# Eight one-bank PSUM tiles and halved transform units in a fused long-convolution and MLP kernel

## The chip, the cores and the metric

The kernel runs on one core of a Trainium2 chip. The core has TensorE (PE in the profile, with PEld for its weight loads), VectorE (DVE), ScalarE (ACT), GpSimd (POOL) and SyncE (SP, which issues most DMAs here). The metric is the device time of one execution in microseconds, the median of the runs. The profile shows one execution, whose span runs from the first to the last instruction.

## The reference

Two blocks follow each other on 2048 positions of 640 channels, in bfloat16. The first is a gated long convolution, the second an MLP; both have a layer norm ahead and a residual around them.

```python
def _A_ref(q, k, v, shift_k, ssm_k, ssm_D):
    ...
    for t in range(ks):                                   # ks = 4
        k_shift = k_shift + k_pad[:, t:t + S, :] * shift_k[:, ks - 1 - t][None, None, :]
    kv = k_shift * v
    ...                                                   # FFT convolution of kv with ssm_k, length 2*S
    y = irfft(rfft(kv_pad) * rfft(kf_pad))[:, 0, :S, :]
    y = y + kv * ssm_D[None, None, :]
    return q * y

def _B_ref(x, w1, b1, w2):                                # w1: 640 x 1728, w2: 1728 x 640
    h = jnp.einsum("bsd,df->bsf", x, w1) + b1
    act = h * jnp.tanh(softplus(h))
    return jnp.einsum("bsf,fd->bsd", act, w2)

h = x + _A_ref(_layernorm(x), A_k, A_v, A_shift_k, A_ssm_k, A_ssm_D)
h2 = h + _B_ref(_layernorm(h), B_w1, B_b1, B_w2)
```

## The kernel before

The convolution is done by a two-stage transform with matmuls against tables. The 2048 positions are split as 128 x 16. Channels are worked on in five blocks of 128 (index b or m), which form three chunks: blocks 0 and 1, blocks 2 and 3, block 4.

The stages, by the names that the order uses:

- `k1pe`, `k1ev`, `dadd`: a block of the filter (`d_n`, 512 KB each) is transposed on PE (16 transposes), evicted from PSUM, and the skip term D is added to its first row.
- `ktpe`, `ktev`, `ktsh`: the same for the keys (`d_k`, four loads).
- `kspe`, `kv`: the 4-tap shift as matmuls with banded weights `wsh`, and on DVE the product with v (`d_v`).
- `s1kpe`/`s1kev` and `s1vpe`/`s1vev`: the first transform stage of filter and kv. A unit is eight pairs of matmuls; the two of a pair write PSUM partitions 0 to 63 and 64 to 127 (cosine and sine). One unit fills 1024 fp32 columns, and one eviction empties it.
- `s2kpe`/`s2kev`, `s2vpe`/`s2vev`: the second stage, one matmul for each of 128 frequencies against the table G (`d_g`, eight loads of 512 KB). For the filter all five blocks go in one matmul of 160 columns; for V each chunk has its own, of 64, 64 and 32 columns.
- `sw`: DMAs that copy the filter's transform with rows swapped in pairs; `p2` and `p1`: the products of transforms on DVE.
- `i1pe`/`i1ev`: the first inverse stage, 320 matmuls of 128 columns. `i2pa`, `i2pb`, `i2pc` and `y`: the second, for each tile of 128 positions (t2 = 0 to 15), one matmul pair for each chunk, evicted together as 640 columns.
- `ln1`, `ln1p`, `lnx` (statistics, scale and application of the first layer norm), `wb`, `h` (gate and residual), `bn`, `pow`, `hc` (the second layer norm), then a transpose: on PE for units 0 and 1 (`trpe`, `trev`), by DMA for the others (`trd`).
- The MLP works in five units of 256, 256, 512, 512 and 512 positions. `m1pe` is the first matmul: 14 blocks of 128 inner rows (1728 padded to 1792 with zeros, `w1z`), five matmuls over the channels each; two blocks share a PSUM tile. `hb` is Mish with bias on ACT. `m2pe` is the second matmul, 2 x 14 matmuls of 320 columns for each tile, `res` the residual add on DVE, `d_out` the store.

PSUM is four tiles of 1024 fp32 columns, two banks each, in one ring (`R_PS`) that all stages share. `ev` is the common eviction helper, so all casts from PSUM stand in the profile at line 367 (ACT) or 369 (DVE).

The order of the work is written out by hand as a list, `ORDER`. A word names an operation and its engine: `t` PE, `a` ACT, `v` DVE, `p` POOL, `d` SP's DMA queue (in the changed kernel also `s`, ACT's DMA queue). `_schedule` walks the list once, gives each operation a planned start from the plan's own durations and its dependencies, picks the PSUM tile that comes free first, and the operations are then emitted by planned start; each engine runs its own in that order.

Buffers are shared over time: G's table makes room for w1 and the transposed layer norm, rn (filter blocks) for the swapped copies and then for w2, uv (V's transform) for the MLP's inner values.

Of the kernel before, what the change touches and what calls it, by code (L numbers as in the profile page):

```python
# [11 lines left out]
ALU = mybir.AluOpType  # L12
# [14 lines left out]
d_id:d d_n1:d cz:v d_n2:d wz:v wm:t cfpe:t coef:v k1pe1:t k1pe2:t k1ev2:v warm:a d_n0:d k1ev1:a k1pe0:t k1ev0:v d_n4:d k1pe4:t k1ev4:v kz:p wsh1:p  # L27
dadd1:p dadd2:p s1kpe2_0:t s1kpe2_1:t s1kpe2_2:t s1kev2_1:v d_a12:d d_k2:d dadd4:p s1kpe2_3:t s1kev2_0:a s1kev2_2:a s1kpe4_2:t d_k0:d s1kpe1_1:t
s1kev2_3:a d_n3:d s1kev4_2:v s1kpe4_0:t s1kpe1_0:t d_k1:d d_x0:d s1kev1_1:a dadd0:p wsh3:p s1kpe4_3:t s1kpe0_3:t s1kev4_0:v s1kev1_0:a d_k3:d
s1kev0_3:a s1kev4_3:v s1kpe4_1:t s1kev4_1:a k1pe3:t k1ev3:v ln1_2:v s1kpe0_1:t s1kpe0_2:t s1kev0_1:a s1kpe1_3:t ktpe1_0:t ktpe0_0:t ln1_1:v s1kev0_2:a  # L30
ktpe1_1:t s1kev1_3:a ktpe0_1:t ktpe1_2:t ktpe0_2:t ktpe2_0:t ktpe1_3:t d_v1:d ktpe0_3:t d_g6:d d_v0:d ktev1:v ktpe2_1:t ktpe3_0:t ktev0:a dadd3:p
ktpe2_2:t ktpe3_1:t ktpe2_3:t ktpe4_0:t ktev2:a ktpe3_2:t ln1_3:v ktsh0:p wsh0:p ktpe4_1:t ktpe3_3:t d_g7:d d_g3:d d_g2:d ktpe4_2:t ktpe4_3:t
s1kpe3_3:t ktev3:v s1kpe1_2:t s1kev3_3:a s1kpe0_0:t s1kpe3_0:t s1kev1_2:a ktev4:v ktsh4:p ktsh1:p s1kev0_0:v ln1_0:v s1kpe3_2:t s1kev3_0:a s1kpe3_1:t
kspe0_1:t s1kev3_1:a ln1p0:p kspe0_0:t s1kev3_2:a kspe4_0:t s2kpe_16:t s2kev_16:a kv0_1:v kv0_0:v kspe4_1:t kv4_0:v s2kpe_9:t s2kev_9:a kv4_1:v
kspe1_0:t s2kpe_6:t s2kev_6:a s2kpe_20:t kspe1_1:t d_g5:d d_g4:d d_g0:d ktsh2:p ln1p3:p wsh2:p kv1_0:v ktsh3:p s2kpe_18:t s2kev_20:a s2kpe_17:t
s2kev_18:a kv1_1:v s2kev_17:a kspe3_1:t s2kpe_8:t s2kev_8:a s2kpe_15:t kv3_1:v s1vpe0_3:t s2kev_15:a s1vpe1_0:t kspe3_0:t s2kpe_21:t s1vev0_3:v
s1vev1_0:a s2kpe_14:t kv3_0:v s2kev_21:a s2kpe_13:t s2kev_14:a s2kpe_19:t s2kpe_0:t s2kpe_11:t s2kev_13:v s2kev_19:a s2kev_0:a s2kpe_10:t s2kev_10:a
d_g1:d s2kpe_4:t s2kpe_12:t s2kev_11:v s2kev_4:v s2kev_12:a s1vpe1_1:t s1vev1_1:v s1vpe0_0:t s1vpe0_2:t s1vev0_2:v s1vpe0_1:t s1vpe1_3:t s1vev0_0:a
s1vev0_1:a s1vev1_3:a s1vpe1_2:t s1vev1_2:v s1vpe3_0:t s2kpe_1:t s1vev3_0:a s2kpe_2:t s2kpe_3:t s2kev_2:a s2kev_1:v kspe2_0:t s2kpe_7:t s2kev_3:v
s2kpe_5:t s2kev_7:a kv2_0:v sw0_1:d kspe2_1:t s2kev_5:a s2vpe0_4:t kv2_1:v s2vpe0_7:t s2vev0_4:a s2vpe0_1:t s2vev0_1:a s2vpe0_2:t s2vev0_2:a  # L40
s2vev0_7:v p2_0_4:v s1vpe4_3:t s2vpe0_3:t s2vev0_3:a s2vpe0_5:t s1vev4_3:v s2vpe0_6:t s2vev0_6:a s1vpe3_2:t s1vev3_2:a s2vev0_5:v p1_0_4:v p2_0_5:v
s1vpe2_1:t p2_0_6:v s1vev2_1:v p2_0_7:v s1vpe2_2:t s1vev2_2:a sw0_0:d s1vpe4_2:t s1vpe3_3:t s1vev4_2:a s1vev3_3:a s1vpe3_1:t s1vpe4_0:t s1vev4_0:v
s1vpe2_3:t p2_0_1:v p2_0_2:v s1vpe2_0:t s1vev3_1:a s1vev2_0:a s1vpe4_1:t s1vev2_3:a s2vpe0_0:t s2vpe1_7:t s2vev0_0:a s2vpe1_5:t s2vev1_7:a s2vev1_5:a
s2vpe1_2:t s2vpe1_0:t s2vev1_0:a s2vpe1_4:t s2vev1_4:a s1vev4_1:a p1_0_5:v p1_0_6:v p1_0_2:v p1_0_1:v sw1_0:d p2_0_0:v s2vev1_2:v p2_1_0:v p2_0_3:v
p1_0_0:v sw1_1:d p1_0_7:v p1_0_3:v p2_1_4:v s2vpe1_3:t s2vpe1_6:t s2vpe1_1:t d_x2:d sw2_1:d s2vev1_6:a s2vpe2_3:t s2vev1_3:a p2_1_3:v s2vev1_1:a
s2vev2_3:a s2vpe2_2:t p2_1_7:v p2_1_6:v p1_1_0:v i1pe0_1:t i1ev0_1:a p2_1_5:v p2_1_1:v s2vpe2_1:t s2vev2_1:a s2vev2_2:a sw2_0:d p2_1_2:v p1_1_4:v
p1_1_2:v p1_1_1:v p1_1_3:v p1_1_6:v p1_1_7:v i1pe0_2:t i1pe0_0:t i1ev0_0:a i1pe0_7:t i1ev0_7:a s2vpe2_0:t i1ev0_2:a i1pe0_4:t i1ev0_4:a s2vev2_0:a
i1pe0_6:t i1ev0_6:a i1pe0_3:t p1_1_5:v i1ev0_3:a i1pe0_5:t i1ev0_5:a i1pe1_2:t i1pe1_0:t i1pe1_6:t i1ev1_0:a i1ev1_6:a i1pe1_1:t i1ev1_1:a i1pe1_7:t
p2_2_2:v p1_2_2:v p2_2_3:v d_w11:d d_w13:d i1ev1_2:a i1ev1_7:a p2_2_1:v p2_2_0:v p1_2_1:v p1_2_0:v i1pe1_4:t i1ev1_4:a p1_2_3:v ln1_15:v ln1_11:v
ln1_12:v i1pe2_2:t i1pe1_3:t i1ev2_2:v i1ev1_3:a i1pe2_0:t i1pe2_1:t i1ev2_1:v i1ev2_0:a i1pe1_5:t ln1_13:v d_w14:d d_t2m:d d_w12:d i1pe2_3:t d_x1:d  # L50
i1ev1_5:a d_w10:d d_w2:d i2pa0:t i2pa1:t i2pb0:t i2pa2:t i2pb1:t i1ev2_3:a i2pc0:t y0:a i2pc1:t d_small:p y1:v b1pe:t i2pb2:t ln1p2:p i2pc2:t w1z:p
ln1p1:p gate:p lnx0:p c_b1:a y2:a lnx1:p i2pa9:t i2pa3:t i2pb9:t i2pc9:t y9:a i2pb3:t i2pa12:t i2pc3:t y3:a i2pb12:t i2pa7:t i2pc12:t y12:a i2pb7:t
i2pa4:t i2pc7:t y7:a lnx3:p ln1p15:p lnx2:p wb1:v wb0:v i2pb4:t i2pa13:t h0:v h1:v bn0:v ln1p13:p pow0:p i2pc4:t y4:a bn1:v i2pb13:t i2pa5:t i2pc13:t
y13:a i2pb5:t i2pa14:t i2pc5:t hc0:v i2pb14:t trpe0:t pow1:p y5:a wb2:v hc1:v i2pc14:t y14:a i2pa10:t trpe1:t i2pb10:t trev0:v i2pa15:t wb3:v i2pa11:t
# [12 lines left out]
res9:v hb4_5:a res8:v m2pe14:t m2pe15:t res14:v m2pe13:t d_out7:d d_out9:d d_out5:d d_out11:d d_out1:d res13:v res15:v d_out13:d d_out14:d m2pe12:t
res12:v d_out15:d d_out10:d d_out8:d d_out12:d
# [15 lines left out]
class _Ring:  # L84
    def __init__(self, bufs):
        self.held = [None] * bufs

    def free(self):
        best = None
        for i, rt in enumerate(self.held):  # L90
            t = 0.0
            for u in rt.users if rt is not None else ():
                if not u.done:
                    break
                t = max(t, u.finish + u.lat + _TAIL[u.eng] + _HOP)
            else:
                if best is None or t < best[0]:
                    best = (t, i)
        return best


class _RT:


    def __init__(self, ring):
        self.ring = ring
        self.users = []
        self.tile = None


class _Op:
    def __init__(self, name, opts, deps, allocs, uses, emit, prio, lat):
        self.name = name
        self.opts = opts
        self.deps = [d for d in deps if d is not None]
        self.allocs = list(allocs)
        for rt in list(allocs) + list(uses):
            rt.users.append(self)
        self.emit = emit
        self.prio = prio  # L120
        self.lat = lat
        self.finish = None
        self.start = None
        self.eng = None
# [732 lines left out]
```

## Time and profile before

| | before |
|---|---|
| median of 3 runs | 230.85 us (230.8 to 232.55) |
| profiled execution | 229.75 us |
| its span | 227.9 us |
| granted TensorE clock | 0.999 |
| PE busy | 217.6 us, 2718 matmuls |
| DVE busy | 143.4 us |
| ACT busy | 132.5 us |
| POOL busy | 51.6 us |
| DMA | 30.60 MB |

Busy time of PE counts a matmul from its start to its modelled end; matmuls overlap in the pipeline, so a busy PE need not be at its peak. How fast an engine really works is read from the spacing of starts in an unbroken series. On ACT and DVE, too, one instruction may start while the one before still drains.

### The profile page before, as it was taken

What the parts mean: (1) busy time and instruction counts of PE and PEld (TensorE: products, weight loads), DVE (VectorE), ACT (ScalarE), POOL (GpSimd) and SP (SyncE); (2) the same over time, 40 slices, a digit from 0 to 9 for tenths busy, and PEclk for the clock granted to TensorE, in tenths of its full rate; (3) what the DMA queues carried; (4) which work ended last, traced back from release to release, by engine and by line L of the source; (5) the groups of instructions that cost most, each with busy time, mean ns of one, the idle gap of its engine ahead of it and who ended that gap; (6) DMA issues with size and microseconds to landing.
All of it is one profiled execution on the core that took longest, in us unless ns stands there. A gap on an engine that the chain in (4) does not pass through costs nothing.

```text
span 227.9 us, 6283 instructions
## 1 busy us (share of the span) xinstructions
PE 217.6 (95%) x2718; PEld 164.6 (72%) x2718; DVE 143.4 (63%) x289; ACT 132.5 (58%) x180; POOL 51.6 (23%) x87
## 2 busy tenths in 40 slices
PE   7989999999879999989999999999999999999993
PEld 2889899999768999878877754445567766447772
DVE  0697998999999999899999998810202120002121
ACT  2388979989999999878966004748240004244000
POOL 0550675000000546149852113210000000000000
PEclk9999999999999999999999999999999999999999
DMA  6999991066898495930001421442200100000304
GB/s 189 417 396 423 415 405 39 4 186 171 250 265 237 109 344 183 384 126 1 3 0 29 83 64 20 69 91 58 58 0 3 58 0 3 0 0 1 117 4 169
DMA packets 27086, 30.60 MB, mean 134 GB/s; under 512 B 9201, under 2 KB 23474, under 8 KB 26674
## 3 DMA queue, kind: packets, MB, share of 16 engines
q1 hardware_dynamic: 26944, 30.19, 40.7%
q8 instruction: 21, 0.34, 0.7%
q14 instruction: 7, 0.06, 0.1%
q10 hardware_dynamic: 50, 0.01, 0.0%
q0 software_dynamic: 64, 0.00, 0.0%
HBM read 20.37 MB, written 2.62 MB: 101 GB/s over the span
## 4 chain that ended last, share of the span: by engine, by line
PE 79%; ACT 9%; DVE 5%; DMA 3%; issue 2%; SPq 1%; POOL 0%; DVEq 0%; ACTq 0%
PE ps L807 27%; PE ps L789 27%; ACT uv L367 7%; PE ps L654 4%; PE ps L653 4%; PE ps L460 4%; DMA rn<-in_A_ssm_k_dram 3%; PE ps L566 2%; PE ps L490 2%; ACT uk L367 2%; PE ps L713 2%; PE ps L513 2%; PE ps L461 2%; DVE uv L369 2%; PE ps L602 2%
## 5 line engine op out<-in xcount | busy, mean ns | idle before, releaser
L797 ACT ACTIVATE uv<-ps,b1s 128x512 bf16<-128x512 f32 (+1 forms) x70 | 36.5, 608 | 59.8 <-PE ps L789 59.8
L789 PE MATMUL ps<-G 128*128 128x512 bf16 (+1 forms) x350 | 62.5, 336 | 0.0
L807 PE MATMUL ps<-rn,uv 128*128 128x320 bf16 x448 | 61.8, 299 | 0.0
L807 PEld LDWEIGHTS <-uv 128*128 128x128 bf16 x448 | 43.8, 98 | 17.5
L789 PEld LDWEIGHTS <-G 128*128 128x128 bf16 x350 | 34.1, 98 | 25.8
L367 ACT CAST uk<-ps 128x1024 bf16<-128x1024 f32 (+2 forms) x50 | 46.6, 1093 | 6.3 <-PE ps L461 3.8
L814 DVE TENSOR_TENSOR xa<-ps,xa 128x640 bf16<-128x640 f32 x6 | 4.9, 823 | 49.0 <-PE ps L807 49.0
L367 ACT CAST uv<-ps 128x1024 bf16<-128x1024 f32 x30 | 28.5, 1095 | 0.0
L653 PE MATMUL ps<-a,uv 128*128 128x128 bf16 x160 | 18.7, 219 | 0.0
L653 PEld LDWEIGHTS <-uv 128*128 128x128 bf16 x160 | 17.8, 113 | 0.1
L738 POOL TENSOR_TENSOR r<-ve,mhalf 128x1 f32<-128x1 f32 x16 | 9.5, 595 | 28.5 <-DVE ve L735 28.4
L814 DVE TENSOR_TENSOR xb<-ps,xb 128x640 bf16<-128x640 f32 x6 | 4.9, 823 | 17.1 <-PE ps L807 14.9
L692 POOL TENSOR_TENSOR r<-ve,mhalf 128x1 f32<-128x1 f32 x16 | 12.7, 797 | 6.9 <-DVE ve L688 6.8
L602 PE MATMUL ps<-uv,G 128*128 128x64 bf16 (+1 forms) x384 | 12.6, 187 | 1.7 <-ACT uv L367 1.7
L369 DVE CAST uk<-ps 128x1024 bf16<-128x1024 f32 (+1 forms) x12 | 13.9, 1191 | 0.4 <-ACT uk L367 0.2
L602 PEld LDWEIGHTS <-G 128*128 128x128 bf16 x384 | 11.7, 96 | 2.4 <-issue 2.2
L617 DVE TENSOR_TENSOR uv<-uv,uk 128x1024 bf16<-128x1024 bf16 x20 | 12.6, 688 | 0.1
L519 DVE TENSOR_TENSOR ra<-ps,rb 128x1024 bf16<-128x1024 f32 x10 | 11.7, 1218 | 1.0 <-PE ps L514 1.0
L369 DVE CAST uv<-ps 128x1024 bf16<-128x1024 f32 x10 | 12.0, 1220 | 0.3 <-PE ps L461 0.2
L460 PE MATMUL ps<-cst,ra 128*64 128x128 bf16 x160 | 10.8, 219 | 1.1 <-ACT uv L367 0.8
L461 PE MATMUL ps<-cst,ra 128*64 128x128 bf16 x160 | 11.0, 221 | 0.0
L713 PE MATMUL ps<-uk,ra 128*128 128x256 bf16 (+1 forms) x96 | 10.7, 255 | 0.2
(103 smaller groups left out, 337.3 us busy)
## 6 DMA issues: line engine op xcount, KB each, us to landing
G<-tab_g SPq DMA_DIRECT2D x8, 512.0 KB, 13.5
rn<-in_A_ssm_k_dram SPq DMA_DIRECT2D x5, 512.0 KB, 5.6
ra<-in_A_k_dram SPq DMA_DIRECT2D x4, 640.0 KB, 7.6
rb<-in_A_v_dram SPq DMA_DIRECT2D x2, 1280.0 KB, 11.0
G<-in_B_w_dram SPq DMA_DIRECT2D x5, 432.0 KB, 6.1
rn<-in_B_w_dram SPq DMA_DIRECT2D x1, 2080.0 KB, 11.5
rn<-uk SPq DMA_DIRECT2D x4, 512.0 KB, 6.5
rb<-uk SPq DMA_DIRECT2D x8, 256.0 KB, 7.7
```

What stands on the lines that cost most here:

```text
L367: nc.scalar.copy(o, i)
L369: nc.vector.tensor_copy(o, i)
L460: nc.tensor.matmul(ps[0:64, dgl, :], lhs, mc, start=True, stop=True)
L461: nc.tensor.matmul(ps[64:128, dgl, :], lhs, ms, start=True, stop=True)
L602: nc.tensor.matmul(ps[:, fl * st:fl * st + n], g_v[:, f0 + fl, :], V[c.i][:, :, f0 + fl, :], start=True, stop=True)
L617: nc.vector.tensor_tensor(v, v, K[c.i][:, :, f0:f1, :], ALU.mult)
L653: nc.tensor.matmul(pz[:, dgl, :], V[c.i][:, dg // 4, :, dg % 4], a12[:, 0, :], start=True, stop=False)
L692: nc.gpsimd.tensor_tensor(r1[:, t2:t2 + 1], ve1[:, t2:t2 + 1], mhalf[:, 0:1], ALU.pow)
L713: nc.tensor.matmul(py[:, o:o + w], t2m[:, t2, ri, :], Z[c.i][:, ri * NT + t2, o - c.c0:o - c.c0 + w], start=(ri == 0), stop=(ri == 1))
L789: nc.tensor.matmul(ph[:, i * 512:i * 512 + w], w1[:, dc, fc * P:fc * P + P], lnhT_of(u)[:, dc, 0:w], start=(dc == 0), stop=(dc == NDC - 1))
L797: nc.scalar.activation(hb_of(u)[:, fc, 0:w], rt.tile[:, i * 512:i * 512 + w], ACT.Mish, bias=b1s[:, fc:fc + 1], scale=1.0)
L807: nc.tensor.matmul(po[:, a * 512:a * 512 + 320], hb_of(u)[:, fc, tl * P:(tl + 1) * P], w2[:, fc, a * 320:a * 320 + 320], start=(fc == 0), ...
```

## The change

- **PSUM.** Eight tiles of 512 fp32 columns (one bank each) instead of four of 1024; the ring `R_PS` has eight places.
- **Halves.** A helper `unit` makes each transform unit as two halves, x and y, each with its own PSUM tile, matmuls and eviction. This holds for filter and key transposes, shift, both forward stages and the first inverse stage. In the second inverse stage the first two chunks (512 columns) and the third (128) have their own evictions, `y..a` and `y..b`. The MLP's first matmul evicts each block of 128 rows by itself; the second is two halves of 320 columns for each tile, with two residual adds (448 and 192 columns for the last tile, each stored by itself).
- **V's second stage joined.** Chunks 1 and 2 share one buffer and one matmul of 96 columns for each frequency.
- **Last 64 inner rows.** The 14th block is no longer padded. Its 64 rows are computed for two groups of positions at once, in the two column halves of PE: units 0 and 1 together, the halves of unit 2, units 3 and 4 together (`m1pex`, `hbx`). Its rows of w2 are held twice, for either half (`w2h`), with zeros in the other rows, so the second matmul keeps 14 steps.
- **First filter block in halves.** Block 1 is loaded as two DMAs of 64 partitions and transposed and evicted as two halves (`k1pe1a`, `k1pe1b`).
- **Also in the diff:** the constants `cst` are loaded from ACT's queue instead of SP's; the warm-up has 7 matmuls instead of 10; the products `p1` and `p2` may run on POOL, and six of them (chunk 0) do, each behind a small copy (`turn`) that orders it after DVE's last product; the list is written anew.

Core of the diff:

```diff
-    banks = [psum.tile([P, 1024], F32, name=f"ps{i}") for i in range(4)]
+    banks = [psum.tile([P, 512], F32, name=f"ps{i}") for i in range(8)]
...
-    uv = [big.tile([P, P * c.ng], BF16, name=f"uv{c.i}") for c in CHUNKS]
+    uv = [big.tile([P, P * n], BF16, name=f"uv{i}") for i, n in enumerate((64, 96))]
...
+    def unit(pe_name, ev_name, dur, evs, cols, deps, pe, evf, ns=2):
+        pes, outs = [], []
+        for h in range(ns):
+            rt = _RT(R_PS)
+            x = "xy"[h] if ns == 2 else ""
+            pes.append(OP(pe_name + x, ("pe", dur / ns), ..., allocs=[rt], emit=lambda e, rt=rt, h=h: pe(ps_f32(rt), h)))
+            outs.append(OP(ev_name + x, evs(cols // ns), pes[-1:] + [o_warm], uses=[rt], emit=lambda e, rt=rt, h=h: evf(e, rt.tile, h)))
+        return pes, outs
...
-        for _ in range(10):
+        for _ in range(7):
             nc.tensor.matmul(ps[:, 0:512], wz[:, 0:P], wz[:, P:D], start=True, stop=True)
...
+    def emit_act_dmas(e):
+        nc.scalar.dma_start(cst[:], dram["cst"])
...
+    def emit_kn1(h):
+        return lambda: nc.sync.dma_start(raw_n[1][64 * h:64 * h + 64], A_ssm_k.rearrange("(d m l) s -> m d l s", m=NDC, l=4)[1, 16 * h:16 * h + 16])
...
+            def pe(ps, h, gi=gi):
+                ps = ps.rearrange("p (g f) -> p g f", g=4)
+                for k in range(4):
+                    q = gi * 8 + h * 4 + k
                     lhs = kk_s[dc][:, q * 64:q * 64 + 64] if which else kv_all[:, dc * S + q * 64:dc * S + q * 64 + 64]
+                    nc.tensor.matmul(ps[0:64, k, :], lhs, mc, start=True, stop=True)
+                    nc.tensor.matmul(ps[64:128, k, :], lhs, ms, start=True, stop=True)
...
+    for x, (nf, n) in enumerate(((16, 64), (10, 96))):
+        for f0 in range(0, P, nf):
+            ...
+                    nc.tensor.matmul(ps[:, fl * n:fl * n + n], g_v[:, f0 + h * kf + fl, :], VX[x][:, :, f0 + h * kf + fl, :], start=True, stop=True)
...
+    for x, us in enumerate(((0, 1), (2,), (3, 4))):
+        w = UNITS[us[0]] // (3 - len(us))
+        ...
+                for h in range(2):
+                    rhs = lnhT_of(us[h])[:, dc, 0:w] if len(us) == 2 else lnhT_of(us[0])[:, dc, h * w:h * w + w]
+                    nc.tensor.matmul(ph[64 * h:64 * h + 64, 0:w], w1[:, dc, 13 * P:FF], rhs, start=(dc == 0), stop=(dc == NDC - 1))
...
-            for a in range(2):
-                for fc in range(NFC): ... w2[:, fc, a * 320:a * 320 + 320]
+            for a, (d0, d1) in enumerate(((0, 448), (448, D)) if t2 == NT - 1 else ((0, 320), (320, D))):
+                    for fc in range(NFC - 1):
+                        nc.tensor.matmul(po[:, 0:d1 - d0], hb_of(u)[:, fc, tl * P:(tl + 1) * P], w2[:, fc, d0:d1], start=(fc == 0), stop=False)
+                    nc.tensor.matmul(po[:, 0:d1 - d0], lhs, w2h[:, d0:d1] if h else w2[:, 13, d0:d1], start=False, stop=True)
...
         for o in order:
+            if o.behind is not None and o.behind.probe is not None:
+                nc.gpsimd.tensor_copy(turn[:], o.behind.probe)
```

Parts of the new list that the prediction speaks of:

```diff
+p2_0_2:p p1_0_2:p p2_0_1:p s1vpe4_0y:t ... s2vev0_6x:v p1_0_0:v p1_0_1:v sw0_1:d ...
+... i2pa0:t i2pa1:t i2pb0:t i2pb1:t i2pa4:t i1ev2_2y:v i2pc0:t y0a:a ...
+hc7:v res0a:v trd6:d ln1_13:v lnx10:a m2pe0b:t m2pe3a:t ... m2pe2a:t trd7:d m1pe2_12:t hb2_12:a ...
+m1pe3_11:t m1pex2:t hb3_5:a m1pe4_2:t ... d_out15a:d d_out8:d d_out14:d d_out15b:d
```

More of the change, by code (lines that the diff above doesn't have):

```diff
@@ L43 @@
[L43 to L54, printed above, removed]
@@ L86, in __init__, with when, take @@
         self.held = [None] * bufs
-    def free(self):
[L89 to L99, printed above, removed]
+    def when(self, i):
+        t = 0.0
+        for u in self.held[i].users if self.held[i] is not None else ():
+            if not u.done:
+                return 1e9
+            t = max(t, u.finish + u.lat + _TAIL[u.eng] + _HOP)
+        return t
+    def free(self):
+        t = [self.when(i) for i in range(len(self.held))]
+        i = min(range(len(t)), key=lambda i: t[i])
+        assert t[i] < 1e9
+        return t[i], i
+    def take(self, i, rt):
+        rt.slot = i
+        self.held[i] = rt
 class _RT:
@@ L145, in _schedule @@
     port = fetched = 0.0
+    last = None
     count, mark = 0, _MARK
@@ L171, in _schedule @@
             port = o.finish
+            if eng == "dve":
+                last = o
+            elif o.probe is not None:
+                o.behind = last
         for rt in o.allocs:
-            rt.slot = rt.ring.free()[1]
-            rt.ring.held[rt.slot] = rt
+            rt.ring.take(rt.slot, rt)
         order.append(o)
@@ L293 @@
     b1s = cpool.tile([P, NFC], F32, name="b1s")
+    hbx = cpool.tile([P, 256 + 256 + 512], BF16, name="hbx")
+    w2h = cpool.tile([P, D], BF16, name="w2h")
     gt = big.tile([P, P * P], BF16, name="G")
@@ L474 @@
     p_ops = [[] for _ in CHUNKS]
-    ks_pe_all, kv_ops, s1_k = [], [], {}
+    ks_pe_all, kv_ops, s1_k = [], [[] for _ in range(NDC)], {}
     def chunk_of(b):
```

467 lines of the change are left out of this document (265 added, 202 removed).

## The prediction

> **What bounds the kernel now.** I read the page, then the stretches by stage, the chain that ended last, and single engines' timelines. The page:
>
> ```profile
> PE 217.6 (95%) x2718; PEld 164.6 (72%) x2718; DVE 143.4 (63%) x289; ACT 132.5 (58%) x180; POOL 51.6 (23%) x87
> DVE  0697998999999999899999998810202120002121
> ACT  2388979989999999878966004748240004244000
> ```
>
> The shares mislead: PE's 95% counts the depth of its pipeline, and DVE and ACT are full for the first half and nearly empty in the second. The stretches (length, then busy time of PE, PEld, DVE, ACT, POOL) show two limits:
>
> ```profile
> 9.80:16.00 6.20, 5.93 (x164) 5.49 (x165) 5.92 (x6) 4.35 (x5) 3.21 (x4) 1.00 1.02 403
> 25.00:38.00 13.00, 12.40 (x260) 11.81 (x258) 12.06 (x14) 11.22 (x13) 10.12 (x15) 1.00 0.77 303
> 52.00:69.00 17.00, 14.34 (x426) 13.05 (x423) 17.00 (x24) 17.00 (x20) 0.00 (x0) 1.00 0.88 241
> 134.00:224.30 90.30, 90.25 (x543) 52.95 (x541) 22.41 (x53) 26.27 (x43) 4.99 (x9) 1.00 0.17 41
> ```
>
> Up to 69 us the two engines that empty PSUM (ACT and DVE) set the pace: both are busy 17.00 of 17.00 from 52 to 69, with gaps only before about 45. From 69 on it is PE: first the inverse transform (i1), then, without a gap, the MLP. The chain of waits says the same:
>
> ```profile
> 91.14 1.09 PE ps L713 x10
> ...
> 133.28 23.74 PE ps L789 x110
> ...
> 224.28 0.82 DVE xb L814
> ```
>
> So the span is the time until the second inverse stage (i2) starts, 91.1 us, plus PE's work behind it (131.6 us by my count, 133.1 with its small gaps), plus 3.6 us of tail. I price the change in these three pieces.
>
> **First piece: until i2.** Halves add instructions, not columns. Ahead of i2pa0 the order lists of the diff have 82 evictions on ACT and 39 on DVE before, 159 and 85 after. What one more eviction costs is the part of it that doesn't grow with columns, read from the spacing of starts in full series on ACT:
>
> ```profile
> 39.54 1.08 ACT L367 CAST uv<-ps 128x1024 bf16<-128x1024 f32 x1
> 40.44 1.38 ACT L367 CAST uk<-ps 128x320 bf16<-128x320 f32 x2
> 40.77 1.90 ACT L367 CAST uk<-ps 128x960 bf16<-128x960 f32 x2
> 42.56 2.71 ACT L367 CAST uk<-ps 128x960 bf16<-128x960 f32 x3
> 43.41 1.86 ACT L367 CAST uk<-ps 128x960 bf16<-128x960 f32 x2
> ```
>
> 1024 columns hold ACT 0.90 us (39.54 to 40.44), 320 hold it 0.33 (to 40.77), 960 hold it 0.85 (42.56 to 43.41), though each shows a longer duration: one starts while the last drains. The line through them is 0.07 us plus 0.81 ns a column, so 512 columns should cost 0.485 us and a split 0.07. No cast of 512 columns is in the trace; below, the split can't cost less than nothing, and the far end is the nearest row of that shape, the Mish of 512 columns (L797): eight in 4.73 us with 0.69 for the last, 0.577 each. I take the line, since it is the same operation. DVE by the same reading: six L519 in 6.88 us with 1.22 for the last, 1.13 each for 1024 columns; a 640-column cast 0.74 (119.32 to 120.06); so 0.09 fixed. Added: 77 x 0.07 = 5.4 us on ACT and 46 x 0.09 = 4.1 on DVE.
>
> Taken off DVE in this piece: six products of chunk 0 go to POOL, 6 x 0.60 = 3.6 us (L617 and L621 in series), and three statistics (ln1_12, ln1_13, ln1_15) go behind i2, 3 x 1.23 = 3.7. Sum over both engines 9.5 - 7.3 = +2.2, or **+1.1 us** on each.
>
> The start: cst leaves SP's queue for ACT's, so the first filter block is issued at 0.73 instead of 1.15, **-0.4 us**. Its halves make the first transposes earlier too, but the new order does the transposes of all four first blocks ahead of the first transform unit, as before, and those blocks arrive at the pace of the DMA engines, busy 0.98 of 3 to 9.8 us. So the halves themselves I price at nothing; the cover is that load stream. The second set of 16 weight loads (1.08 us more on PE) is hidden there too. The shorter warm-up (7 for 10 matmuls, 1.3 us) goes with the block's earlier arrival.
>
> What finer units should buy is idle time. Between 9.8 and 91 us (81.2 us) the stretches add up to 75.3 us busy on ACT and 77.1 on DVE, so 10 us of idle, 5.0 on each, nearly all before 52. The waits name it: ACT for PE at L461, at L566 and at the change from one transform to the next, DVE for L514 and for the last filter block. With eight tiles an eviction can begin after four column pairs, not eight, and PE may run seven units ahead instead of three; the order fills the change of transforms with key transposes. Bounds: nothing gained (the gaps are late loads and dependencies) and all 5.0. I take half, **-2.5 us**.
>
> V's joined second stage saves 128 of 384 matmuls: 64 of the 32-column ones take 1.88 us, so 128 cost 3.8, while widening the 64-column ones to 96 adds about 2. The 1.8 us are worth nothing while ACT and DVE are full (52 to 69); if that cover went, they would be a gain. The i1 stage stays as long as it was: 320 matmuls at 0.0556 us (two rows of L653 start 0.11 apart with one of L654 between) are 17.8 us, plus 1.3 us of V's remainder instead of two groups of 0.80. So i2 is earlier only if i1 starts earlier. Sum of this piece: 1.1 - 0.4 - 2.5 = **-1.8 us**, bounds +0.7 and -4.3.
>
> The queues that move: the weight loads d_w1 still wait for the last second-stage matmul; d_x1 now stands behind d_w2 on SP, which has one more transfer of 80 KB. It then lands some 5 us after i1 ends; its first user, ln1_4, has 10.9 us of DVE work ahead of it from i2's start. Hidden, with about 6 us to spare. On POOL, d_small and the w2h memset come ahead of the six products; POOL sat idle from 37 to 76 us.
>
> **Second piece: PE behind i2.** The 14th block of 64 rows now costs 5 matmuls in each of five units: 2 x 5 x 0.109 + 3 x 5 x 0.216 = 4.33 us (ten L789 of 256 columns take 1.09, twenty of 512 take 4.32). As column pairs it costs half, if a pair runs at once. The first transform shows that such pairs do:
>
> ```profile
> 11.05 0.22 PE L460 MATMUL ps<-cst,x 128*64 128x128 bf16 x1
> 11.05 0.22 PE L461 MATMUL ps<-cst,x 128*64 128x128 bf16 x1
> 11.10 0.22 PE L460 MATMUL ps<-cst,x 128*64 128x128 bf16 x1
> ```
>
> Both halves start together and the next pair 0.055 us later, the pace of one matmul of 128 columns. That saves 2.16 us. Going in and out of the halves costs about 0.09 each time (last transpose at 10.81, first pair at 10.97, where 0.067 was its pace), six times, 0.5. Net **-1.6 us**, bounds 0 and -2.2. [...]
>
> The second MLP matmul stays 448 long; its halves are the same two runs of 14. The residual adds double to 32 at 320 columns: 16 x 0.09 = 1.4 us more on DVE, which is under 2 tenths busy there. What could be late is the layer norm of tiles 4 to 7 that m1pe2 waits for: before, its last DMA transpose is issued by 130.5 us and lands about 2.6 later, m1pe2 starts at 133.28, so it is just in time. In the new order DVE has 30.8 us of work from i2 to hc7 instead of 33.9, PE 38.4 instead of 40.7: the margin grows by about 1 us. I price it at nothing; late DVE would show as a PE gap there, microsecond for microsecond. m1pex2 waits for tiles 12 to 15; m1pe4 and all that PE has left queue behind it, but other m1pe4 blocks stand ahead of it and wait for the same tiles.
>
> **Third piece: the tail.** PE ends at 224.28 and the span at 227.9: 0.82 us of residual add over 640 columns, 0.33 of issue, the rest landing. The last piece is 192 columns now: 0.09 + 0.195 plus the drain, about 0.4 us. With the smaller transfer **-0.6 us**, bounds -0.4 and -0.9.
>
> **Sum:** -1.8 - 1.6 - 0.6 = -4.0 us on a span of 227.9, so 223.9, and 225.75 for the profiled execution (229.75; 1.85 lie around its span). The runs have a median of 230.85, 1.1 above the profiled one; I carry that over: **226.85 us**, 1.7% less. A measurement here tells about 1% from no change.
>
> **Rivals.**
>
> (1) All idle goes: the engines run full from about 11 us on, as they do from 52 to 69. Another -2.5: 224.3 us. For it: no wait over 0.7 us after 45 us even with four tiles. Against: filter blocks and G still come by a full DMA stream until 34 us.
>
> (2) The halves buy no idle time, because the gaps are late loads and the drain between stages. Then the first piece is +0.7 and the sum -1.5: 229.35 us, no change that can be told.
>
> (3) POOL is late. Six products there cost about 1.9 us each (2.07 for 1120 columns, L417), 11.4 in a row, and DVE, in order, stops at p1_0_1, which needs the last of them; behind it queue the products of chunk 0 that i1 waits for and evictions of V. The list leaves DVE 7.1 us of work from the first to there. If POOL starts no earlier than the list has it, DVE loses 11.4 - 7.1 = 4.3 us: 231.15. Against: the swapped copy of K that POOL needs is issued some 11 us of work before, so POOL can start 3 us sooner. POOL's own exposure is real in the trace:
>
> ```profile
> 76.79 4.00 POOL L692 TENSOR_TENSOR r<-ve,mhalf 128x1 f32<-128x1 f32 x1
> ```
>
> This takes 0.55 us elsewhere and stood still while DVE multiplied. But the order keeps DVE on PSUM casts meanwhile, and those kept their 1.13 us beside POOL's L417 at 13.2.
>
> (4) **Slower:** a half doesn't follow the line. If a cast of 512 columns holds ACT 0.577 us, as the Mish does, ACT pays 159 x 0.092 = 14.6 us more ahead of i2, of which 2.5 fit into its remaining idle time: +12.1, 239 us. The forecast's gain is used up from 0.041 us a half, (4.0 + 2.5)/159. Against: four widths lie on one line, and Mish carries a bias operand. [...]
>
> (5) The pairs don't overlap at 256 and 512 columns: 2.2 us lost, 229 us.
>
> **Chances.** Forecast 0.5, (1) 0.25, both faster by over 1%. (2) 0.11, (3) 0.05, (5) 0.02 within 1%. (4) 0.07. That gives faster 0.75, same 0.18, slower 0.07. The range runs from all bounds met at once (-4.3 - 2.2 - 0.9 = -7.4: 223.4), a little under it for a first half that packs tighter than counted, to rival (3): 222.5 to 231.2.
>
> **What would show it.** Right: i2 (the first matmul on t2m) starts near 89.3; series of 512-column casts on ACT 0.49 apart; ACT and DVE together idle some 5 us between 10 and 89; the 64-column pairs of the MLP starting together; from the first MLP matmul to the last no gap on PE over 1 us; 3 us from PE's end to the span's. Wrong: casts over 0.53 apart (rival 4), DVE waiting for POOL before i1 (3), a PE gap ahead of unit 2's first MLP matmul, or i2 at 91 or later with the casts as priced (2).

## The result, and the profile after

The changed kernel takes 228.87 us (median of 20 runs, 227.55 to 230.67) against 230.53 for the kernel before on the same chip: a ratio of 0.9925, 95% interval 0.9902 to 0.9948. That is 0.75% less, where 1.7% less was forecast. The interval leaves out no change at all, but the difference is under the 1% that the prediction named as what a measurement can tell. Its profiled execution has a span of 226.4 us (before: 227.9).

The page of the changed kernel, the totals and the slices of DVE and ACT:

```profile
PE 216.7 (96%) x2608; PEld 164.9 (73%) x2608; DVE 149.0 (66%) x351; ACT 133.8 (59%) x266; POOL 63.3 (28%) x94
DVE  0489799999999999888999898675820000002422
ACT  2188699999999999899786025730206357400000
```

ACT has 266 instructions where it had 180, and DVE 351 where it had 289: the halves. From 28 us to about 85 both digits stand at 9; before, a few 7s and 8s stood among them up to 51 us. The first six slices together are no fuller than before. The stretches shown in the prediction, now:

```profile
9.80:16.00 6.20, 6.20 (x130) 6.04 (x130) 4.55 (x11) 4.64 (x7) 3.27 (x5) 1.00 1.02 408
25.00:38.00 13.00, 12.73 (x255) 12.45 (x254) 12.43 (x23) 12.05 (x25) 2.33 (x4) 1.00 0.82 316
52.00:69.00 17.00, 15.91 (x389) 14.34 (x386) 16.93 (x31) 17.00 (x37) 15.84 (x10) 1.00 0.71 193
134.00:223.30 89.30, 89.28 (x554) 52.67 (x552) 30.48 (x82) 26.03 (x42) 8.25 (x15) 1.00 0.18 43
```

After the stretch come PE, PEld, DVE, ACT and POOL busy with their counts, the granted clock, the DMA share and GB/s. Between 25 and 38 us ACT is 0.8 us fuller, but between 9.8 and 16 us DVE has 4.55 busy us where it had 5.92. A window that overlaps the second stretch lost more; before first, then after:

```profile
20.00:30.00 10.00, 9.40 (x197) 8.97 (x198) 9.20 (x21) 9.28 (x10) 4.29 (x6) 1.00 1.01 413
```

```profile
20.00:30.00 10.00, 7.97 (x216) 7.57 (x211) 8.52 (x15) 8.07 (x18) 7.33 (x14) 1.00 0.88 330
```

PE, DVE and ACT are all less busy there. The chain of waits of the changed kernel has the three marks of the prediction: the first matmul on t2m (L788), the first MLP matmul (L883), and the last work on PE (L900).

```profile
93.12 3.08 PE ps L788 x30
...
101.68 3.87 PE ps L883 x35
...
220.22 1.77 PE ps L900 x13
```

i2 starts 2.0 us later than before (93.12, was 91.14). PE's last matmul ends at 223.28 (before: 224.25), so its stretch behind i2 is 130.16 us, 2.95 less. The tail is 3.11, 0.58 less. Sum: +1.98 - 2.95 - 0.58 = -1.55, the whole difference of the spans. **So the pieces behind i2 brought what was forecast and more; the piece ahead of it, forecast at -1.8, went the other way.**

### The profile page after: what moved, and what is told of

It reads as the page before. It is cut to its first block, busy times and chain, and to the rows that moved or that the text cites. A ratio compares the mean times of both kernels' runs of the same rounds, so it can differ in the third digit from the quotient of the medians.

```text
span 226.4 us, 6281 instructions
## 1 busy us (share of the span) xinstructions
PE 216.7 (96%) x2608; PEld 164.9 (73%) x2608; DVE 149.0 (66%) x351; ACT 133.8 (59%) x266; POOL 63.3 (28%) x94
## 4 chain that ended last, share of the span: by engine, by line
PE 81%; ACT 8%; DVE 4%; DMA 2%; issue 2%; SPq 1%; ACTq 0%; DVEq 0%
PE ps L883 25%; PE ps L900 25%; ACT uv L415 6%; PE ps L788 4%; PE ps L523 4%; PE ps L728 3%; PE ps L645 3%; PE ps L729 3%; DVE uv L417 3%; PE ps L619 3%; PE ps L550 2%; DMA rn<-in_A_ssm_k_dram 2%; ACT uk L415 2%; PE ps L901 2%; PE ps L569 2%
## 5 line engine op out<-in xcount | busy, mean ns | idle before, releaser
L900 PE MATMUL ps<-rn,uv 128*128 128x320 bf16 (+2 forms) x416 | 61.0, 299 | 0.0
L883 PE MATMUL ps<-G 128*128 128x512 bf16 (+1 forms) x325 | 58.9, 337 | 0.0
L900 PEld LDWEIGHTS <-uv 128*128 128x128 bf16 x416 | 40.5, 98 | 16.8
L415 ACT CAST uk<-ps 128x512 bf16<-128x512 f32 (+1 forms) x91 | 47.5, 706 | 3.1 <-PE ps L524 2.6
L883 PEld LDWEIGHTS <-G 128*128 128x128 bf16 x325 | 31.2, 98 | 23.6 <-issue 0.6
L415 ACT CAST uv<-ps 128x512 bf16<-128x512 f32 (+2 forms) x63 | 33.2, 859 | 0.0
L906 DVE TENSOR_TENSOR xa<-ps,xa 128x320 bf16<-128x320 f32 x12 | 5.5, 484 | 40.4 <-PE ps L901 40.4
L417 DVE CAST uk<-ps 128x512 bf16<-128x512 f32 (+1 forms) x32 | 20.1, 678 | 1.3 <-ACT uk L415 0.4
L574 DVE TENSOR_TENSOR ra<-ps,rb 128x512 bf16<-128x512 f32 x20 | 12.5, 684 | 0.2
L417 DVE CAST uv<-ps 128x512 bf16<-128x512 f32 (+1 forms) x19 | 11.8, 681 | 0.0
L645 PE MATMUL ps<-uk,G 128*128 128x160 bf16 x128 | 11.5, 230 | 0.0
L415 ACT CAST rb<-ps 128x512 bf16<-128x512 f32 (+1 forms) x26 | 11.0, 475 | 0.9 <-PE ps L788 0.7
L523 PE MATMUL ps<-cst,ra 128*64 128x128 bf16 x160 | 11.1, 219 | 0.3
```

The lines of the kernel that those rows point to most:

```text
L415: nc.scalar.copy(o, i)
L417: nc.vector.tensor_copy(o, i)
L523: nc.tensor.matmul(ps[0:64, k, :], lhs, mc, start=True, stop=True)
L574: nc.vector.tensor_tensor(kv_w[:, m, :, 8 * h:8 * h + 8, l0:l0 + n], ps.rearrange("p (l t d) -> p d t l", l=n, t=8), raw_v[:, 8 * h:8 * h ...
L645: nc.tensor.matmul(ps[:, o:o + 160], g_v[:, f, :], KA[:, :, f, :], start=True, stop=True)
L883: nc.tensor.matmul(ph[:, 0:w], w1[:, dc, fc * P:fc * P + P], lnhT_of(u)[:, dc, 0:w], start=(dc == 0), stop=(dc == NDC - 1))
```

## The experiments

The question was what made the start 3.8 us worse than forecast. All ratios are to the kernel before. For each profiled execution the table splits the time until i2 in two: the work is half of what ACT and DVE are busy until then, the idle time is the rest. "First pair" is the start of the first pair of the first transform.

| kernel | ratio (95%) | first pair | i2 starts | work | idle |
|---|---|---|---|---|---|
| before | 1 | 10.97 | 90.98 | 79.23 | 11.75 |
| changed | 0.9925 (0.9902 to 0.9948) | 13.13 | 92.96 | 80.22 | 12.73 |
| changed, ten warm-ups | 0.9909 (0.9885 to 0.9933) | 10.97 | 92.71 | 80.16 | 12.55 |
| changed, whole first block | 0.9817 (0.9795 to 0.984) | 10.84 | 91.40 | 79.98 | 11.42 |
| whole, ten warm-ups | 0.9818 (0.9796 to 0.9841) | 10.75 | 91.16 | 80.04 | 11.12 |
| the same, 32 more instructions | 0.985 (0.983 to 0.9871) | 10.70 | 91.61 | 80.02 | 11.59 |
| the same, transfer in halves | 0.9878 (0.9857 to 0.99) | 11.34 | 92.28 | 80.06 | 12.22 |
| the same, V's load late | 0.9769 (0.9749 to 0.9789) | 11.09 | 90.41 | 79.95 | 10.46 |
| before, with halves alone | 1.0082 (1.0059 to 1.0104) | 11.38 | 93.88 | 82.90 | 10.98 |

(Here i2 is the first matmul of its line, 0.16 us ahead of the chain's entry.)

**Ten warm-up matmuls.** The transposes of the changed kernel run slowly at the start:

```profile
1.26 3.17 PE L443 MATMUL ps<-hc 128*128 128x512 bf16 x7 [1.26 <-DVE warm L433]
4.56 2.22 PE L604 MATMUL ps<-cst,rn 64*128 64x64 bf16 x32
7.73 1.94 PE L619 MATMUL ps<-cst,rn 128*128 128x128 bf16 x16 [0.95 <-DMA rn<-in_A_ssm_k_dram]
```

Sixteen whole transposes take 1.94 us, 0.107 apart, and the first pair of the first transform comes 2.2 us later than before. The first suspect was the warm-up:

```diff
-        for _ in range(7):
+        for _ in range(10):
             nc.tensor.matmul(ps[:, 0:512], wz[:, 0:P], wz[:, P:D], start=True, stop=True)
```

> The changed kernel with ten warm-up matmuls in place of seven; nothing else differs. Theory (clock): seven matmuls, 32 quarter-array transposes and a wait of 1 us leave TensorE at half rate, so the whole-block transposes run 0.105 us apart and the first pair of the first transform starts at 13.1 us. With ten they should run about 0.067 apart, the first pair should start near 11.2, the first matmul on t2m near 91.5 in place of 93.1, and the time should fall by 1 to 2 us below the changed kernel (ratio to the kernel before about 0.985). Rival (front off the path): filter blocks and G come by a full DMA stream to 34 us, so the earlier start is lost in later waits: the first matmul on t2m moves by under 0.4 us, ratio 0.9925 as without it. Rival (halving): the split of the first block costs by itself; the transposes stay at 0.105.

```profile
5.64 1.98 PE L604 MATMUL ps<-cst,rn 64*128 64x64 bf16 x32
7.55 1.21 PE L619 MATMUL ps<-cst,rn 128*128 128x128 bf16 x16
8.70 0.20 PE L463 MATMUL ps<-sk_r,cst 32*128 32x80 bf16 x1
```

The same sixteen take 1.21 us, and the first pair starts at 10.97 as before. But i2 moves by 0.25 us and the ratio by 0.0016, inside both intervals. The theory was right on the transposes and wrong on the time: of 2.2 us gained at 11 us, 0.4 are left at 30. What takes them is a wait of PE on nothing that the profile shows. The two stops of this kernel:

```profile
22.75 0.96 PE L550 MATMUL ps<-cst,ra 128*128 128x128 bf16 x13 [1.50 <-issue]
...
29.22 0.98 PE L550 MATMUL ps<-cst,ra 128*128 128x128 bf16 x13 [1.66 <-issue]
```

The changed kernel's own stops are 1.76 us (to 24.54) and 0.27 (to 29.64), so 1.1 of the 2.2 us go into longer stops.

**Seven warm-up matmuls in the kernel before.** The edit is the reverse, in the old kernel.

> The kernel before with seven warm-up matmuls in place of ten; nothing else differs. Theory (clock): the transposes of the filter blocks (0.067 us apart) slow to about 0.1, the first pair moves from 10.97 to 12.5 or later, and the time rises by 1 to 2 us (ratio 1.004 to 1.009). Rival (front off the path): ratio 1.000 +- 0.002, though the transposes may be slower. Rival (halving): the transposes stay at 0.067, ratio 1.000.

Ratio 1.0044 (1.0016 to 1.0071), 1.0 us; by the medians 0.4 (231.2 against 230.81). Its 64 filter transposes, in one row, start at 5.48 and take 5.80 us. They are 0.107 apart until 8.8 us and 0.062 from there on, yet the first pair comes only 0.24 later. By the ratio the loss lies at the foot of the clock theory's range, by the medians below it; a slow start of the transposes is not free there, but its price stays uncertain.

**The first filter block whole again,** with seven and with ten warm-up matmuls:

```diff
-d_go:d d_n1a:d wz:v wm:t d_n1b:d d_n0:d ... k1pe1a:t k1pe1b:t ... k1ev1a:v k1ev1b:v dadd1b:v ... dadd1a:p
+d_go:d d_n1:d wz:v wm:t d_n0:d ... k1pe1x:t k1pe1y:t ... k1ev1x:v k1ev1y:v ... dadd1:p
```

> The changed kernel with the first filter block whole again (one transfer, two units of eight 128x128 transposes, one addition of the D row), still with seven warm-up matmuls. Theory (clock, too few warm-up matmuls): still about 0.1 us a transpose, first pair near 13, ratio near 0.9925. Rival (halving: 64x64 transposes keep TensorE cold): transposes at 0.067, first pair near 11.3, ratio about 0.985.

> The changed kernel with ten warm-up matmuls and the first filter block whole: the start as it was before, everything else changed. Theory (clock): transposes at 0.067, first pair near 11, the first matmul on t2m near 91 to 91.5, ratio about 0.985; if the halves of the first block were worth anything, it is slower than ten warm-ups with the halved block by up to 1 us. Rival (front off the path): 0.9925.

0.9817 and 0.9818: the halved block costs about 1% (2.3 to 2.5 us by the medians, 226.35 and 226.6 against 228.87), and with the block whole the number of warm-up matmuls makes no difference. With seven of them the first pair starts at 10.84, not near 13: the transposes are 0.107 apart only until 6.0 us, where in the changed kernel it is until 12.8. So seven warm-up matmuls by themselves don't explain the late start; each of these is one execution, and what sets the moment stays open.

The place of the stops explains part of the 1%. With the whole block and ten warm-ups:

```profile
22.54 0.24 PE L523 MATMUL ps<-cst,xa 128*64 128x128 bf16 x1 [1.30 <-issue]
...
27.06 0.30 PE L644 MATMUL ps<-uk,G 128*128 128x160 bf16 x2
28.67 2.53 PE L644 MATMUL ps<-uk,G 128*128 128x160 bf16 x34 [1.30 <-issue]
```

Count PE's instructions in the order up to each stop, a matmul and its weight load as one each. With the halved block the first stop comes with 13 of the 16 transposes of ktpe2y and ktpe0y left: after 700 instructions. With the whole block it comes three matmuls into s1kpe0_3x: 700 as well. The second comes after 956 (13 of 24 transposes of ktpe left) and 954 (two matmuls into the second stage). So PE stops at the same instruction, 256 apart (within the two of the count), whatever it executes; the 32 instructions that the halves add (16 transposes and 16 weight loads) push work from ahead of the stop to behind it. The second stage of the filter starts at 27.06 with the whole block and at 30.04 with the halved one. The page of the changed kernel lists a queue for instructions:

```profile
q8 instruction: 20, 0.33, 0.6%
```

Twenty packets of 16 KB; the kernel before, with 220 more instructions on PE, has 21. From 99.20 us on, where PE has no wait in the changed kernel, the packets start 242 to 258 of PE's instructions apart, so one goes with each such step. A stop lasts 1.3 to 1.7 us in the versions of the changed kernel with ten warm-ups and a DMA share of 1.0 from 20 to 30 us.

**32 more instructions and nothing else,** and **the transfer in halves and nothing else,** both on the kernel with ten warm-ups and the whole block:

```diff
-        for _ in range(10):
+        for _ in range(7):
             nc.tensor.matmul(ps[:, 0:512], wz[:, 0:P], wz[:, P:D], start=True, stop=True)
+        for _ in range(19):
+            nc.tensor.matmul(ps[:, 0:80], wz[:, 0:P], wz[:, P:P + 80], start=True, stop=True)
```

> The changed kernel with the first filter block whole and ten warm-up matmuls, of which the last three (1536 columns) are cut into 19 of 80 columns (1520 columns): 32 more instructions on TensorE (16 matmuls and their weight loads, as many as the halved block adds) in about the same time. Theory (code delivery: while the DMA stream is full, TensorE gets its instructions in blocks of some 250, one in about 6.3 us, and stops at the same instruction numbers, near 700 and 945, whatever it executes): the two stops come 32 instructions earlier in the program, the first second-stage matmul of K starts near 30.0 us in place of 27.1 with a stop at 28.7, the first matmul on t2m about 1.3 us later (92.4), ratio to the kernel before 0.988 against 0.982. Rivals (the transfer in halves, or the half transposes themselves, cost the time): the same as without, 0.982.

```diff
-d_go:d d_n1:d wz:v wm:t d_n0:d
+d_go:d d_n1a:d wz:v wm:t d_n1b:d d_n0:d
```

> The changed kernel with ten warm-up matmuls, the first filter block transferred in two halves of 64 rows but transposed whole. Theory (code delivery): as with the whole transfer, ratio 0.982, the first matmul on t2m near 91.2. Rival (the halved transfer costs: by 25 us the changed kernel had moved 0.3 MB less than the one with the whole block): the later blocks land about 0.7 us later, the first matmul on t2m near 92.5, ratio 0.988 to 0.991.

```profile
21.87 1.02 PE L551 MATMUL ps<-cst,ra 128*128 128x128 bf16 x13 [1.69 <-issue]
...
28.07 1.01 PE L551 MATMUL ps<-cst,ra 128*128 128x128 bf16 x13 [1.31 <-issue]
```

With 32 cheap instructions added, the stops fall into the same transposes with the same number left as in the halved kernel: again after 700 and 956. That settles what the stops count. The price of 32 instructions was over-guessed: 0.985, 0.7 us by the ratio (0.0032; the intervals overlap) and 0.45 us at i2, not 1.3; the second stage starts at 28.92, not 30.0. The stops ended 0.6 to 0.7 us earlier than without (21.87 for 22.54, 28.07 for 28.67), which gave part of it back.

The halved transfer alone gives 0.9878, 1.4 us more than whole, with i2 1.1 later; the code theory had expected nothing. The two kernels' first 9 us, halves first:

```profile
0.00:9.00 9.00, 6.38 (x44) 3.59 (x45) 2.20 (x5) 1.56 (x3) 0.20 (x4) 1.00 0.80 247
```

```profile
0.00:9.00 9.00, 7.13 (x53) 4.23 (x54) 2.31 (x5) 2.17 (x3) 0.61 (x5) 1.00 0.79 270
```

At the same busy share the engines moved 247 GB/s instead of 270, that is 0.2 MB less in 9 us, or half a microsecond at the 408 of the full stream (changed kernel, 9.8 to 16 us); the first pair starts 0.6 later. One pair of traces would be little, but the other versions of the changed kernel agree: in the same window the two others with halves have 256 and 258 GB/s, the seven others with the transfer whole 263 to 284. Why transfers of 64 rows are slower there was not tried.

**Halved transposes alone,** the transfer whole, on the changed kernel with ten warm-ups (its `k1pe1a` and `k1pe1b` wait for one `d_n1`):

```diff
-d_go:d d_n1a:d wz:v wm:t d_n1b:d d_n0:d
+d_go:d d_n1:d wz:v wm:t d_n0:d
```

> The changed kernel with ten warm-up matmuls and the first filter block transferred whole, but transposed in two halves of 16 transposes of 64x64 each, as the change has it. With the transfer also whole in its transposes the ratio was 0.982, with both halved 0.991. Theory (three costs add: the halved transfer 0.9 us, 32 more instructions 0.4 us, the rest the 16 more transposes' own time): 2.3 - 0.9 = 1.4 us over the whole block, ratio 0.988. Rival (the halves cost only together, by the wait between them): ratio 0.984 or less.

0.9864 (0.9832 to 0.9895), 1.1 us over the whole block. The intervals overlap, but on the same chip all six runs (227.23 to 228.51 us) lie above all four of the whole block (226.09 to 226.64). With the transfer's 1.4 this makes 2.5, against 2.1 for both by the ratios (0.9909 - 0.9818): they add, within the intervals. So each half of the edit costs something by itself. How much of the transposes' part is the 32 instructions (0.7 above) and how much their own time is not separated. In its profiled execution the granted clock is 0.50 from 22.8 to 26.1 us, behind a stop of 1.96, so its i2 start is not in the table.

**V's load behind x's.** On the kernel with the whole block and ten warm-ups:

```diff
-... d_g6:d s1kev2_3x:a s1kev3_2y:a d_v1:d s1kpe0_2y:t ... d_x0:d s2kpe_12x:t
+... d_g6:d s1kev2_3x:a s1kev3_2y:a s1kpe0_2y:t ... d_x0:d d_v1:d s2kpe_12x:t
```

> The changed kernel with the first filter block whole and ten warm-up matmuls, and the load of the first half of V (1.28 MB, some 3.2 us of the DMA stream) moved on SP's queue from 17 us to behind the load of x at 27 us. Theory (code delivery slowed by the full DMA stream): the stream ends some 3 us earlier, near 23.7, so the stop of 1.3 us at 28.7 goes and the first one at 22.5 may shorten; the first matmul on t2m 0.8 to 1.3 us earlier (near 90.1), ratio about 0.977. Rival (the stops have another cause, or V is then late): no gain, or a wait of kspe for V after 31 us; ratio 0.982 or above.

The same window before and after this edit:

```profile
23.00:30.00 7.00, 5.70 (x139) 5.47 (x134) 5.17 (x9) 5.86 (x11) 1.90 (x4) 1.00 1.02 396
```

```profile
23.00:30.00 7.00, 7.00 (x164) 6.91 (x159) 6.20 (x11) 6.84 (x14) 2.23 (x4) 1.00 0.67 235
```

With the DMA share down to 0.67 PE has no idle time there; the second stop is gone and the first is 1.13. The ratio is 0.9769 as expected, the i2 start 90.41 (expected 90.1). With a median of 225.34 us this is the fastest version, ahead of both kernels.

The traces also hold every DMA packet with its queue and its start, which ties the stops to the code directly. Start and end of the second and the third packet of q8, and the moment at which PE goes on behind instruction 700 and behind about 956:

| kernel | second packet | PE goes on | third packet | PE goes on |
|---|---|---|---|---|
| changed | 22.01 to 23.09 | 24.54 | 27.32 to 28.38 | 29.64 |
| changed, ten warm-ups | 20.20 to 21.28 | 22.75 | 26.69 to 27.75 | 29.22 |
| whole, ten warm-ups | 20.00 to 21.09 | 22.54 | 26.17 to 27.18 | 28.67 |
| the same, 32 more instructions | 19.49 to 20.52 | 21.87 | 25.55 to 26.62 | 28.07 |
| the same, V's load late | 20.44 to 21.53 | 22.76 | 24.84 to 25.94 | no stop |

Every stop ends 1.2 to 1.5 us after a code packet has landed. In the three middle rows, under the full stream (a DMA share of 1.0), the third packet starts 3.6 to 3.9 us after PE goes on behind 700; with V's load late (0.67 from 23 to 30 us) it is 2.1, and the packet has landed 1.5 us before PE comes to that place, at 27.43. So it is the code that PE waits for, and at the second stop the full stream that makes it late. What a packet waits for before it starts is not shown.

With seven warm-up matmuls instead:

> The changed kernel with the first filter block whole and V's load behind x's (ratio 0.977 with ten warm-up matmuls), with seven. Theory (the start is paced by code blocks, so a cold TensorE at 5 us is hidden): the same, 0.977 +- 0.002. Rival (clock: with the stops shortened the cold start shows): slower by 0.5 to 1 us, ratio 0.980.

0.9801 (0.9771 to 0.983); the intervals overlap, so whether the shorter warm-up costs time again once the stops are shorter stays open. In its profiled execution the transposes of the filter are 0.062 apart from their first on, so it had no slow start, and still i2 starts 1.3 us later, at 91.73.

**The halves alone in the kernel before:** its list with each unit as two neighbours, V's later stage not joined, no pairs, the whole block.

```diff
-s1kpe1_3:t ... s1kev1_3:v
+s1kpe1_3x:t s1kpe1_3y:t ... s1kev1_3x:v s1kev1_3y:v
```

> The kernel before with the eight one-bank tiles and every transform unit in halves, and nothing else of the change: its order with each unit as two adjacent halves, V's later stage not joined, the 64 rows padded, the first block whole, ten warm-up matmuls. Theory (a half costs what the line through the widths says, and the idle time of ACT and DVE is late loads and code, not the size of a unit): 123 added evictions at 0.07 and 0.09 us are 9.5 us of two engines, 4.8 each, of which some is taken from idle time: the first matmul on t2m 2 to 4 us later, ratio 1.010 to 1.018. Rival (finer units let the two engines run full): the idle time pays it, the first matmul on t2m within 1 us of before, ratio under 1.005.

1.0082, 1.9 us slower, i2 2.9 later: between the two expectations. The work per engine grows by 3.67 us, 7.3 engine-us for 123 added evictions, 0.06 each, where the prediction had 0.07 and 0.09. The idle time falls by 0.77 us.

**The column pairs taken back,** on the fastest version:

```diff
-        for fc in range(NFC - 1):
+        for fc in range(NFC):
...
-m1pex0:t hbx0:a
+m1pe0_13:t m1pe1_13:t hb0_13:a hb1_13:a
```

> The changed kernel with the first filter block whole, ten warm-up matmuls and V's load behind x's (ratio 0.977), with the last 64 inner rows padded to a 14th block again as before: 25 matmuls in five units in place of 30 that run as column pairs. Theory (a pair runs in the time of one): 4.33 us in place of 2.54, so TensorE's stretch from the first matmul on t2m to its last grows by 1.8 us, from 130.3 to 132.1, the start stays as it is, ratio 0.985. Rival (the 3 us that this stretch lost came with the new order around the first MLP matmuls, or the pairs only share TensorE): it grows by under 0.7 us, ratio under 0.980.

0.9892 (0.986 to 0.9925) against 0.9769. PE's stretch from i2 to its end grows by 2.41 us, where 1.8 was expected, from 130.32 to 132.73: 1.64 of work (130.31 to 131.95 busy), and one wait for an inner activation on ACT, which has two to do where the pair has one:

```profile
182.83 1.46 PE L860 MATMUL ps<-G 128*128 128x512 bf16 x6 [0.78 <-ACT uv L865]
```

In the changed kernel the ten matmuls of the first pair group show as one row; the next matmul starts 0.67 after them, where the ten padded ones took 1.09 before:

```profile
109.65 0.74 PE L863 MATMUL ps<-G 128*64 128x256 bf16 x10
110.32 0.29 PE L788 MATMUL ps<-uk,ra 128*128 128x128 bf16 x2
```

**POOL's six products back on DVE,** on the fastest version (`p2_0_0:p` and five more become `:v`).

> The changed kernel with the first filter block whole, ten warm-up matmuls and V's load behind x's (ratio 0.977), with the six products of chunk 0 that the change gave to POOL (2.12 us each there, 51 to 64 us) back on DVE at their places in the order, 0.69 us each. Theory (until the first matmul on t2m ACT and DVE are the bound, POOL is off the path): 4.1 us more on DVE, shared with ACT only where the order lets it: the first matmul on t2m 2 to 4 us later, ratio 0.986 to 0.994. Rival (POOL's products are late for DVE and i1, or slow DVE by running beside it): no later or earlier than without, ratio 0.977 or less.

0.9913 (0.9884 to 0.9942), i2 3.1 us later: 2.2 more work per engine (4.4 engine-us) and 0.9 more idle time. POOL was not in the way. In the changed kernel it has the last product done just before DVE comes for it, and DVE has no wait there:

```profile
61.91 2.14 POOL L695 TENSOR_TENSOR rn<-rn,uv 128x1024 bf16<-128x1024 bf16 x1
```

## Why the prediction was right or wrong

**The work ahead of i2: right.** Forecast +1.1 per engine, measured +0.99. Casts of 512 columns on ACT follow each other 0.477 us apart in the two series below (the ninth of the second starts at 59.86), where 0.49 was forecast. Two halves hold ACT 0.95 us against 0.90 for a whole, so a split costs 0.05, a little less than the 0.07 of the line and far from the 0.53 us a cast of rival (4):

```profile
42.21 6.23 ACT L415 CAST uv<-ps 128x512 bf16<-128x512 f32 x12
...
56.05 4.70 ACT L415 CAST uv<-ps 128x512 bf16<-128x512 f32 x9
```

**The halved first block, priced at nothing: one of two steps that failed.** It cost 2.1 to 2.5 us by the ratios (0.0091 and 0.0108), more than the change gained, and 1.6 us at i2 (92.96 against 91.40, 92.71 against 91.16). The prediction took an earlier arrival for granted, put the second set of 16 weight loads at nothing because the load stream would cover it, and did not count the extra transfer at the head of that stream. The stream covered neither: the transfer alone cost 1.4 us and the transposes alone 1.1. The shorter warm-up, also priced at nothing, cost nothing that shows in this kernel.

**Half of the idle time removed (-2.5): the other step, and at i2 the larger one.** Halves alone took 0.77 us off, and with the block whole the changed kernel has 0.63 less than before (11.75 to 11.12), which includes the -0.4 for cst. So i2 starts 0.2 us later than before there (91.16), where 1.8 earlier was forecast: 2.0 of the 3.8 us are missing even without the halved block. Rival (2) had the right reason, late loads, but not the right load: beside data it was PE's own code. The trace of before had shown it as well, as two waits of PE on "issue", of 0.65 us to 16.41 and of 0.28 to 28.53, 256 matmuls and their loads apart, and they were passed over as small:

```profile
PE ps L460 <- issue: 0.9, 2, 0.6
```

What remained idle between 20 and 30 us in ACT and DVE could not be had by finer units, since PE gave them nothing: with the whole block and ten warm-ups each of them idles 2.5 us there, and the two stops are 2.6. Rival (2)'s number, 229.35 us, is met as well, but by luck: its first piece of +0.7 came out at +2.0 and its -1.6 for PE at -2.95.

**PE behind i2: -1.6 forecast, -2.95 measured.** The term of the column pairs was right: 1.64 of work. The rows (0.67 us for the pair group, 1.09 for the ten padded ones before) agree with the pace of the first transform, and rival (5) is out. The other 1.3 us was not in the sum: PE had 0.81 us of gaps in this stretch before, 0.01 after, and 0.5 us less work beside the pairs, whose place was not looked for. (The prediction had counted 131.6 us of work and 1.5 of gaps before; the trace has 132.46 and 0.81.) The one gap that the waits of before show:

```profile
98.30 0.45 PE L761 MATMUL ps<-cst,hc 128*128 128x128 bf16 x5 [0.55 <-DVE hc L743]
```

It is the wait of the first MLP transposes for DVE, and in the new order, where the first MLP matmul comes 8.6 us after i2 instead of 9.9, it is gone. Which part of the order closed it was not tried. The layer norms ahead of unit 2 were in time, as priced.

**The tail:** -0.6 forecast, -0.58 measured. **POOL (rival 3):** its products took 2.12 us and not 1.9, and were still in time. **The range** of 222.5 to 231.2 has the result in it, but as a case within 1%, which had 0.18. The sum of -4.0 on the span is nearly what the changed kernel does without its one bad part: with the block whole and ten warm-ups the span is 224.3, 3.6 less. That agreement is luck: there the piece until i2 is 2.0 us worse than forecast, and PE behind i2 is 1.35 better and the tail 0.25.

## What to carry to other kernels

Where the start runs under a full DMA stream, look for PE waits on "issue" and count the instructions between them: if the number is constant (256 here), an earlier start or finer pieces ahead of the stop buy little (here 0.25 of 2.2 us at i2), more instructions cost (here 0.7 us for 32), and thinning the stream buys (here a ratio of 0.9769 against 0.9818). Splitting a load at the head of such a stream is not free just because the parts are smaller (here 1.4 us): price its transfer and every instruction that it adds. A share of idle time may be claimed for a change only when the thing that ends each wait is something that the change touches.

## What the runs showed of the hardware

- PE's stops at the start lay 256 of its instructions apart. In the versions of the changed kernel with ten warm-ups PE stopped for 1.3 to 1.7 us after instruction 700 and about 956 at a DMA share of 1.0, and not at the second place at 0.67. The stops ended 1.2 to 1.5 us after the landing of a 16 KB packet of the instruction queue.
- PE's start-to-start of 128-column transposes was 0.107 us at first and 0.062 later. The change came at 12.8 us in the changed kernel, at 8.8 in the kernel before with seven warm-up matmuls, at 6.0 with seven and the block whole, and with ten at 7.0 or earlier. The profile's granted clock says 1.00 throughout, but the clock records of the first three traces begin only at 12.80, 8.81 and 6.00.
- A transfer of 512 KB as two of 64 rows moved data slower in the first 9 us (247 against 270 GB/s) at the same busy share (0.80 and 0.79); over all versions of the changed kernel 247 to 258 against 263 to 284.
